# A top-32 attention and MLP kernel on one core: the first pair's steps spread over three PSUM banks, one weight product summed as the weights arrive, two pairs prepared in the MLP's bank, and a buffer for each chunk of rows

## The chip, the cores and the metric

The kernel runs on one core of a Trainium2 chip. A core has five engines that run side by side, each through its own queue in order: TensorE (PE, matrix products and transposes, writing to PSUM), VectorE (DVE), ScalarE (ACT), GpSimd (POOL) and SyncE (SP, which here issues nearly all DMAs). The metric is device time in microseconds. The kernel before took 906.09 us (median of three runs, 905.07 to 906.38).

## What is computed

```python
# 8 batches x 8 heads, 576 queries and keys, head size 64
scores = q @ k.T / 8
kth    = the 32nd largest score of the row
attn   = softmax(scores where scores >= kth, else -1e9)
x      = (attn @ v), heads side by side      # 4608 tokens x 512
h      = x @ w_in                             # 512 -> 2048
g      = max(h, 0) + alpha * min(h, 0)        # alpha per column
out    = g @ w_out                            # 2048 -> 512
```

The last three lines are computed as `relu(h) @ (w_out * (1 - alpha)) + x @ (w_in @ (w_out * alpha))`. The second product, `w_in @ (w_out * alpha)`, is a 512 x 512 matrix that does not depend on x. The text calls it the linear matrix; it is made once, on the chip, in the opening of the kernel.

## The kernel before

**Pairs, tiles, ticks.** Two heads of one batch form a pair; there are 32 pairs, four to a batch. Each pair has nine tiles of 128 rows of scores (the ninth holds the last 64 rows of both heads), 288 tiles in all. One Python loop writes the order of all engines by hand, tick by tick; tick n starts tile n. Within a tick each engine gets its instructions in a fixed order, and every engine runs its own list in order. So the engines drift apart, and wait on each other only through data and buffers.

**What a tile goes through.** PE makes scores (`ps`, line 319) one or two ticks ahead. ACT shifts them by the row's threshold guess (`b`, 328), takes a row sum of signs (`h`, 334) and later exponentials (`e`, 339). POOL turns the row sum into a sign bit (`SG`, 344). DVE then flips the tile (`y`, 350), takes six times the eight largest of a segment (`C`, 360), merges them (375, 377), and seven ticks after the tile began compares (`mk`, 424). POOL multiplies (`w`, 434; for the last six tiles DVE does both, 431). SP transposes the weights of two tiles by DMA (`wT`, 447; `wm` in 442 and 443 for ninth tiles), PE multiplies with v (`pu`, 493), DVE takes reciprocals (`rz`, 510) and ACT writes the rows to `xb` (522). In the last batch tiles run across the four pairs, and `av_last`, `rz_last` and `out_last` (493, 539, 546, the last two on DVE) take that place, three ticks after the weights, or two once all tiles have begun.

**Preparing a pair.** `prep_plan(p)` lays out steps at ticks counted from `BASE[p]`: transposes of q and k (`pq`, `pk`, and `pt` for the last 64 rows), a Gram matrix of k (`pg`), its product with q (`pr`, in two pieces of 512 and 64 columns), a product on DVE (`P`, 231), row statistics (`st`), and eight small DVE steps that give the threshold guess `NT0`. Before, `pq`, `pk`, `pt` and `pg` all take turns in one PSUM bank (`ps_a`), so each waits until ACT has copied the one before. `pr`, `st` and the `pu` of the attention product share the two banks of `ps_d`, which are handed out in rotation. Pairs 11 and 20 (`LEAD1`, `LEAD2`) are prepared early, four or five ticks beside another pair.

**Weights and MLP.** `weight_steps` gives PE and ACT one step per tick from tick 0: the rows of w_out are loaded and scaled (595, 596), then, in twelve steps at ticks 35 to 46, four 128 x 512 slices of the linear matrix are summed (`pl`, 603), six, six and four products to a slice, and copied (607). The bank is `ps_m`. When four chunks of `xb` and the chunk `xm` of a batch are written, SP transposes them (`xT`, 556 and 558), and `mlp_steps` feeds blocks of up to 512 tokens: `ph` (644), relu on ACT (650), `pz` (658, 662), copy (667), store (673). The blocks use `ps_m` too; between two feeds there are ticks with no MLP step. `xb` of a batch is one tile of four chunks in a single buffer.

**What sets the order at the end.** In the last batch up to two MLP steps are taken in a tick. After `av_last` of a chunk's second half the chunk is transposed, and its block is fed one tick later.

Of the kernel before, what the change touches and what calls it, by code (L numbers as in the profile page):

```python
# [9 lines left out]
FP32 = mybir.dt.float32  # L10
BF16 = mybir.dt.bfloat16
# [19 lines left out]
def kernel(  # L31
# [10 lines left out]
    nc = tc.nc  # L42
    B, H, S_, D = q.shape
# [7 lines left out]
    TPP = 9  # L51
# [118 lines left out]
    def prep_plan(p):  # L170
        d = pairs[p]
        GK = GKs[p % 2]
        ns = slice(p * TPP, p * TPP + TPP)

        def high(x):
            return x.bitcast(BF16).rearrange("p (n h) -> p n h", h=2)[:, :, 1]

        def pe_q():
            d["qkT"] = qkTs[p % NQ]
            d["pq"] = ps_a.tile([128, 512], FP32, name="pq", tag="pa")  # L180
            for c in range(4):
                nc.tensor.transpose(d["pq"][:, c * 128:(c + 1) * 128], d["q"][:, c, :], ident_f)

# [4 lines left out]
            nc.scalar.copy(d["v"][:, :, 0:D], d["st_v"])  # L188

        def pe_k():  # L190
            d["pk"] = ps_a.tile([128, 512], FP32, name="pk", tag="pa")
            for c in range(4):
                nc.tensor.transpose(d["pk"][:, c * 128:(c + 1) * 128], d["k"][:, c, 1:129],
                                    ident_f)
# [2 lines left out]
            nc.scalar.copy(d["qkT"][:, 1, 0:512], d["pk"])  # L197

        def pe_t():
            d["pt"] = ps_a.tile([128, 2, 64], FP32, name="pt", tag="pa")  # L200
            nc.tensor.transpose(d["pt"][:, 0, :], d["q"][0:64, 4, :], ident_f[0:64, 0:64])
            nc.tensor.transpose(d["pt"][:, 1, :], d["k"][0:64, 4, 1:129], ident_f[0:64, 0:64])

# [1 line left out]
            nc.scalar.copy(d["qkT"][:, :, 512:S], d["pt"])  # L205

        def pe_g():
            d["pg"] = ps_a.tile([128, 130], FP32, name="pg", tag="pa")
            for c in range(5):
                nc.tensor.matmul(d["pg"], high(d["k"][:, c, 1:129]), high(d["k"][:, c, :]),  # L210
                                 start=(c == 0), stop=(c == 4))
# [4 lines left out]
        def pe_r():  # L216
            d["P"] = prep.tile([128, S], BF16, name="P", bufs=1)
            d["pr"] = []
            d["qTb"] = high(d["qkT"][:, 0, :])
            for n0, n1 in ((0, 512), (512, S)):  # L220
                pr = ps_d.tile([128, n1 - n0], FP32, name="pr", tag="pd")
                for r in (slice(0, 64), slice(64, 128)):
                    nc.tensor.matmul(pr[r], GK[r, 1 + r.start:65 + r.start], d["qTb"][r, n0:n1],
                                     start=True, stop=True)
                d["pr"].append((n0, n1, pr))
# [5 lines left out]
                nc.vector.tensor_tensor(d["P"][:, n0:n1], pr, d["qkT"][:, 0, n0:n1], ALU.mult)  # L231

        def pe_s():
            st = ps_d.tile([128, 2, TPP], FP32, name="st", tag="pd")
# [49 lines left out]
        if p == 0:  # L284
            ts = [-16, -15, -14, -13, -12, -11, -9, -8, -8, -8, -8, -8, -8, -8, -8, -8, -2]
        elif p == 1:
            ts = [-9, -8, -7, -6, -5, -4, -3, -2, -2, -2, -2, -2, -2, -2, -1, -1, 1]
        else:
            ts = [-14, -13, -12, -11, -10, -9, -7, -6, -6, -5, -5, -4, -4, -3, -3, -2, -8]
# [3 lines left out]
                 dict(dve=[dve_p]), dict(pe=[pe_s]), dict(act=[act_m]), {dvx: [dve_2]},  # L293
                 dict(dve=[dve_3]), {dvx: [dve_4]}, dict(dve=[dve_5]), {dvx: [dve_6]},
                 dict(dve=[dve_7]), {dvx: [dve_8]}, dict(dve=[dve_9]), dict(act=[act_v])]
        return list(zip(ts, steps))

    tiles = {}
# [186 lines left out]

    def x_tiles(b):
        if b not in xb:
            xb[b] = prep.tile([128, 4, DM], BF16, name="xb", bufs=1)
            xm[b] = prep.tile([64, DM], BF16, name="xm", bufs=1)

    def av_one(o_, d, wT, side, cs):
# [22 lines left out]
    def av_out(p, g):  # L514
        d = pairs[p]
        b, kt = p // KPB, p % KPB
        pu, rz = d["pu", g], d["rz", g]
        for c in range(4 + 2 * g):
            m = 128 if c < 4 else 64
            h0 = 128 * kt + 64 * (c % 2)  # L520
            dst = xb[b][:, 2 * g + c // 2, h0:h0 + 64] if c < 4 else xm[b][:, h0:h0 + 64]
            nc.scalar.activation(dst, pu[0:m, c, 0:D], AF.Copy, scale=rz[0:m, c:c + 1])  # L522

    pul = {}
# [17 lines left out]
    def out_last(i, g):  # L542
        m = 128 if i < 4 else 64
        pu, rz = pul.pop((i, g))
        dst = xb[B - 1][:, i, :] if i < 4 else xm[B - 1]
        nc.vector.tensor_tensor(  # L546
            dst[:, 256 * g:256 * g + 256].rearrange("p (s d) -> p s d", s=4), pu[0:m, :, 0:D],
            rz[0:m, 0:4].unsqueeze(2).to_broadcast([m, 4, D]), ALU.mult)

    def x_turn(b, chunks):  # L550
        for i in chunks:
            c0 = (b * S + 128 * i) % NX
            if b == B - 1:
                c0 = b * S % NX + (64 + 128 * i if i < 4 else 0)
            if i < 4:
                nc.sync.dma_start_transpose(xT[:, :, c0:c0 + 128], xb[b][:, i, :])
            else:
                nc.sync.dma_start_transpose(xT[:, :, c0:c0 + 64], xm[b])

    def weight_steps():  # L560
# [17 lines left out]
        def lin(f):  # L578
            return xT[:, f // 4, DM * (f % 4):DM * (f % 4 + 1)]
# [15 lines left out]
            nc.scalar.activation(w_out_b[:, f, :], ws, AF.Copy, scale=alpha1m[:, f:f + 1])  # L595
            nc.scalar.activation(lin(f), ws, AF.Copy, scale=alpha_sb[:, f:f + 1])

        def w_id(kk, part):
            if part == 0:
                hold["pl"] = ps_m.tile([128, DM], FP32, name="pl", tag="misc")  # L600
            pl = hold["pl"]
            for f in range(6 * part, min(6 * part + 6, NFT)):
                nc.tensor.matmul(pl, hold["inT"][:, kk, f, :], lin(f),
                                 start=(f == 0), stop=(f == NFT - 1))

        def w_id2(kk):
            nc.scalar.copy(w_id_b[:, kk, :], hold["pl"])

        yield alpha, None
        yield (lambda: None), None  # L610
# [1 line left out]
        for f in range(NFT):  # L612
            yield ((lambda f=f: (w_out(f + 2) if f + 2 < NFT else None,
                                 w_in(f // 2) if f < 8 and f % 2 == 0 else None)),
                   (lambda f=f: w_out2(f)))
            yield (lambda: None), (lambda f=f: w_in2(f // 2) if f < 8 and f % 2 == 1 else None)
        for kk in range(NKT):
            for part in range(3):
                yield ((lambda kk=kk, part=part: w_id(kk, part)),
                       (lambda kk=kk: w_id2(kk)) if part == 2 else None)  # L620

    banks = [0, 0]

# [74 lines left out]
    with tc.manual_schedule(engines={E.PE, E.Activation, E.DVE, E.Pool, E.SP}):  # L698
# [19 lines left out]
        def tail_of(n, wn):  # L718
            wp, wj = ORDER[wn]
            b = wp // KPB  # L720
            if wp < P0:
                if wj == 3:
                    put(n + 3, "pe", lambda: av(wp, 0))
                    put(n + 4, "dve", lambda: av_rz(wp, 0))
                    put(n + 6, "act", lambda: av_out(wp, 0))
                    if wp % KPB == KPB - 1 and b >= 5:
                        put(n + 6, "end", lambda: x_turn(b, (0, 1)))
                        put(n + 8, "end", lambda: feed(b * S + 256))
                if wj == 8:
                    put(n + 4, "pe", lambda: av(wp, 1))  # L730
                    put(n + 5, "dve", lambda: av_rz(wp, 1))
                    put(n + 7, "act", lambda: av_out(wp, 1))
                    if wp % KPB == KPB - 1:
                        put(n + 7, "end", lambda: x_turn(b, range(2 if b >= 5 else 0, 5)))
                        put(n + 9, "end", lambda: feed((b + 1) * S))
            elif (wj == 8 or wj % 2) and wp % 2:
                i, g = wj // 2, (wp - P0) // 2
                dt = 3 if n < NT else 2
                put(n + dt, "pe", lambda: av_last(i, g))
                put(n + dt + 1, "dve", lambda: rz_last(i, g))  # L740
                put(n + dt + 1, "dvx", lambda: out_last(i, g))
# [247 lines left out]
```

## Time and profile before

| what | value |
|---|---|
| median of 3 runs | 906.09 us |
| profiled execution, its own time | 906.11 us |
| its span, first to last instruction | 904.2 us |
| DVE busy | 845.1 us (93%) |
| ACT busy | 787.6 us (87%) |
| PE busy | 737.7 us (82%) |
| POOL busy | 430.8 us (48%) |
| mean granted TensorE clock | 0.901 |

The shares are means over the whole run. A row of the timeline gives the start, the length, the engine, the line, and in brackets how long the engine stood idle before it and what released it. Lines are those of the kernel before; a queue of DMA issues is written with a q (SPq).

### The profile page before, as it was taken

How to read it: one execution, taken by the hardware profiler on the slowest of the kernel's cores; microseconds unless marked ns; L12 is line 12 of the kernel's file. 1: busy time of each engine (PE TensorE's matmuls, PEld its weight loads, DVE VectorE, ACT ScalarE, POOL GpSimd, SP SyncE). 2: the span in 40 equal slices, each digit the busy share in tenths (PEclk: the TensorE clock that was granted, in tenths of full speed). 3: DMA queues.
4: the chain of work that ended last, by engine and by line, in shares of the span. 5: the costliest groups of instructions: out<-in, count | busy, mean ns of one | idle time of the engine just before them, and what ended most of it. 6: DMA issues, size and time to landing. Idle time of an engine off the chain costs nothing. (4 is left out here: it accounts for less than half of the span.)

```text
span 904.2 us, 20676 instructions
## 1 busy us (share of the span) xinstructions
PE 737.7 (82%) x5747; PEld 433.0 (48%) x5747; DVE 845.1 (93%) x5305; ACT 787.6 (87%) x1809; POOL 430.8 (48%) x629
## 2 busy tenths in 40 slices
PE   5667697878958789887985879978897979899976
PEld 3344444434534445544453445644455555556663
DVE  3999989999998999999998999999999999989980
ACT  5999989799977998989996999999997999879831
POOL 1465544555454555554544555455545555445510
PEclk9665779699977999989996999999997999899989
DMA  6799644544665454564566445575455663444551
GB/s 153 135 176 205 128 81 90 118 92 93 139 130 95 94 105 114 100 134 89 109 150 112 91 94 112 109 142 92 97 118 105 123 108 87 81 88 88 91 99 33
DMA packets 343019, 99.50 MB, mean 110 GB/s; under 512 B 335200, under 2 KB 335216, under 8 KB 342896
## 3 DMA queue, kind: packets, MB, share of 16 engines
q1 hardware_dynamic: 340544, 95.71, 53.6%
q0 software_dynamic: 1152, 2.10, 1.7%
q8 instruction: 47, 0.77, 0.4%
q14 instruction: 76, 0.62, 0.2%
q10 hardware_dynamic: 1200, 0.30, 0.2%
HBM read 36.71 MB, written 9.44 MB: 51 GB/s over the span
## 5 line engine op out<-in xcount | busy, mean ns | idle before, releaser
L434 POOL TENSOR_TENSOR w<-mk,e 128x576 bf16<-128x576 bf16 x250 | 319.2, 1277 | 360.1 <-DVE mk L424 185.1
L360 DVE MAX8 C<-y 128x8 f32<-128x96 f32 x1728 | 420.5, 244 | 0.1
L319 PE MATMUL ps<-qkT 64*128 64x288 f32 (+1 forms) x1280 | 258.8, 478 | 34.8 <-ACT b L328 34.8
L328 ACT ACTIVATE b<-ps,NT 128x576 f32<-128x576 f32 x288 | 201.8, 758 | 19.3 <-PE ps L319 19.3
L334 ACT ACTIVATE h<-b 128x576 bf16<-128x576 f32 x288 | 202.7, 704 | 1.6
L644 PE MATMUL ph<-xT,w_in_b 128*128 128x128 bf16 (+2 forms) x1088 | 161.8, 299 | 44.7 <-ACT gT L650 34.1
L319 PEld LDWEIGHTS ps<-qkT 64*128 64x128 f32 (+1 forms) x1280 | 136.1, 195 | 96.5 <-ACT b L328 57.7
L339 ACT ACTIVATE e<-b 128x1152 bf16<-128x1152 f32 (+1 forms) x158 | 173.8, 1100 | 0.6 <-POOL w L434 0.6
L375 DVE MAX8 L<-C 128x8 f32<-128x48 f32 x864 | 163.4, 189 | 0.1
L350 DVE TENSOR_SCALAR y<-b,SG 128x576 int32<-128x576 int32 x288 | 147.3, 512 | 6.2 <-POOL SG L344 5.7
L424 DVE TENSOR_SCALAR mk<-b,KP 128x576 bf16<-128x576 f32 x282 | 143.8, 510 | 0.0
L644 PEld LDWEIGHTS <-w_in_b 128*128 128x128 bf16 x1088 | 87.9, 103 | 112.4 <-issue 81.5
L662 PE MATMUL pz<-w_out_b,gT 128*128 128x512 bf16 x576 | 139.6, 380 | 0.0
L650 ACT ACTIVATE gT<-ph 128x512 bf16<-128x512 f32 x144 | 87.9, 618 | 42.1 <-PE ph L644 42.0
L377 DVE MATCH_REPLACE8 C<-L,C 128x48 f32<-128x48 f32 x576 | 108.9, 189 | 0.0
L493 PE MATMUL pu<-v_bf,wT 128*128 128x65 bf16 (+1 forms) x1600 | 70.5, 200 | 29.7 <-DVE P L231 16.9
L493 PEld LDWEIGHTS <-wT 128*128 128x128 bf16 (+1 forms) x1600 | 66.1, 104 | 42.7 <-issue 20.5
L662 PEld LDWEIGHTS <-gT 128*128 128x128 bf16 x576 | 52.8, 98 | 69.2 <-issue 14.0
L344 POOL TENSOR_SCALAR SG<-S_all 128x1 int32<-128x1 f32 x288 | 65.2, 227 | 19.6 <-ACT h L334 19.6
L434 POOL TENSOR_TENSOR wm<-mk,e 128x576 bf16<-128x576 bf16 x32 | 40.8, 1276 | 52.1 <-DVE mk L424 46.6
L334 ACT ACTIVATION_READ_ACCUMULATOR h<-b 128x1 f32 x288 | 62.6, 217 | 0.0
L522 ACT ACTIVATE xb<-pu,rz 128x64 bf16<-128x64 f32 x224 | 53.9, 358 | 3.4 <-DVE C L360 2.5
(100 smaller groups left out, 716.0 us busy)
## 6 DMA issues: line engine op xcount, KB each, us to landing
out_dram<-o_sb SPq DMA_DIRECT2D x35, 256.0 KB, 2.3
st_q<-in_q_dram SPq DMA_DIRECT2D x64, 128.0 KB, 2.9
st_v<-in_v_dram SPq DMA_DIRECT2D x64, 128.0 KB, 2.6
kst<-in_k_dram SPq DMA_DIRECT2D x62, 128.0 KB, 2.8
w_stage<-in_moe_w_out_dram SPq DMA_DIRECT2D x16, 256.0 KB, 3.2
w_in_b<-in_moe_w_in_dram POOLq DMA_DIRECT2D x8, 256.0 KB, 6.6
wT<-w SPq DMA_TRANSPOSE x128, 3.3
st_q<-in_q_dram SPq DMA_DIRECT2D x32, 32.0 KB, 2.8
```

The lines of the kernel that those rows point to most:

```text
L319: nc.tensor.matmul(o_, l_, r_, start=True, stop=True)
L328: nc.scalar.activation(t["b"].rearrange("p (a c) -> p a c", a=2), t["ps"], AF.Identity, bias=NT0[:, p * TPP + j:p * TPP + j + 1], scale=ON ...
L334: nc.scalar.activation(h, tiles[n]["b"], AF.Sign, accum_out=S_all[:, n:n + 1])
L339: nc.scalar.activation(e, tiles[n0]["bu"], AF.Exp, scale=scl)
L350: nc.vector.tensor_scalar(t["y"].bitcast(I32), t["b"].bitcast(I32), FLIP, SG[:, n:n + 1], ALU.bitwise_xor, ALU.bitwise_xor)
L360: return [lambda g=g: nc.vector.max(out=C[:, n % TPP, g, :], in_=t["y"][:, g * SEG:(g + 1) * SEG]) for g in range(NSEG)]
L375: ops.append(lambda r=r, src=src: nc.vector.max(out=L[:, 8 * r:8 * r + 8], in_=src))
L424: nc.vector.tensor_scalar(t["mk"], t["b"], row_limit(n), None, ALU.is_ge)
L434: nc.gpsimd.tensor_tensor(dst, t["mk"], t["e"], ALU.mult)
L493: nc.tensor.matmul(o_, wT[:, 4 * side + c, cs], d["v"][:, 5 * side + c, :], start=(c == 0), stop=(c == 4))
L644: nc.tensor.matmul(hold[f][:, i, :], w_in_b[:, kk, (f + i) * 128:(f + i + 1) * 128], xT[:, kk, c0:c0 + tb], start=(kk == 0), stop=(kk == N ...
L662: nc.tensor.matmul(pz[0:m], hold["gT"][:, f, r0:r0 + m], w_out_b[:, f, :], start=False, stop=(f == NFT - 1))
```

## The change

- In `prep_plan`, a function `bank` now picks the PSUM pool by pair and step. For pair 0, `pq` and `pk` stay in `ps_a`, `pg` goes to `ps_m`, `pt` to `ps_d`. For pairs 11 and 20 all but the second piece of `pr` and `st` go to `ps_m`. For all other pairs nothing moves.
- For pair 0 the steps are regrouped: `pq`, `pg`, `pt` are issued together, their three copies follow, then `pr`, then `pk`; scores still come last.
- The first slice of the linear matrix is summed two products at a time between the weight loads, from step 6 on; one product is left for tick 35. The other three slices take four steps of four products. That is one step more in all, ending at tick 47.
- `xb` becomes four tiles of one chunk each in a rotation of six buffers.
- In the last batch the attention product follows the weights by two ticks throughout. Its rz and out_last, the transpose of the chunk and the feeding of its block move with it.

No operation is added or removed. On PE, DVE, ACT and SP some change places.

```diff
+        def bank(nm, shape):
+            pool, tag = (ps_d, "pd") if nm in ("pr1", "st") else (ps_a, "pa")
+            if nm == "pr0":
+                pool, tag = ps_d, "pd"
+            if p == 0 and nm == "pt":
+                pool, tag = ps_d, "pd"
+            if (p == 0 and nm == "pg") or (p in (LEAD1, LEAD2) and nm not in ("pr1", "st")):
+                pool, tag = ps_m, "misc"
+            return pool.tile(shape, FP32, name=nm, tag=tag)
...
-            d["pq"] = ps_a.tile([128, 512], FP32, name="pq", tag="pa")
+            d["pq"] = bank("pq", [128, 512])
...
-                pr = ps_d.tile([128, n1 - n0], FP32, name="pr", tag="pd")
+                pr = bank(f"pr{n0 // 512}", [128, n1 - n0])
...
+        if p == 0:
+            ts = [-16, -15, -14, -13, -12] + [-11] * 8 + [-2]
+            steps = [dict(pe=[pe_q, pe_g, pe_t]), dict(act=[act_q, act_g, act_t], pe=[pe_r, pe_k]),
+                     dict(dve=[dve_p]), dict(act=[act_k], pe=[pe_s]), dict(act=[act_m])] + steps[8:]
...
-            xb[b] = prep.tile([128, 4, DM], BF16, name="xb", bufs=1)
+            xb[b] = [prep.tile([128, DM], BF16, name="xb", bufs=6) for _ in range(4)]
...
-        def w_id(kk, part):
-            if part == 0:
-                hold["pl"] = ps_m.tile([128, DM], FP32, name="pl", tag="misc")
-            pl = hold["pl"]
-            for f in range(6 * part, min(6 * part + 6, NFT)):
-                nc.tensor.matmul(pl, hold["inT"][:, kk, f, :], lin(f),
+        done = [0]
+
+        def w_id(kk, lim):
+            if done[0] == 0:
+                hold["pl", kk] = ps_m.tile([128, DM], FP32, name="pl", tag="misc")
+            for f in range(done[0], lim):
+                nc.tensor.matmul(hold["pl", kk], hold["inT"][:, kk, f, :], lin(f),
                                  start=(f == 0), stop=(f == NFT - 1))
+            done[0] = lim % NFT
...
-            yield (lambda: None), (lambda f=f: w_in2(f // 2) if f < 8 and f % 2 == 1 else None)
-        for kk in range(NKT):
-            for part in range(3):
-                yield ((lambda kk=kk, part=part: w_id(kk, part)),
-                       (lambda kk=kk: w_id2(kk)) if part == 2 else None)
+            yield ((lambda f=f: w_id(0, min(done[0] + 2, f)) if f >= 6 else None),
+                   (lambda f=f: w_in2(f // 2) if f < 8 and f % 2 == 1 else None))
+        yield (lambda: w_id(0, NFT)), (lambda: w_id2(0))
+        for kk in range(1, NKT):
+            for lim in (4, 8, 12, 16):
+                yield ((lambda kk=kk, lim=lim: w_id(kk, lim)),
+                       (lambda kk=kk: w_id2(kk)) if lim == NFT else None)
...
                 i, g = wj // 2, (wp - P0) // 2
-                dt = 3 if n < NT else 2
+                dt = 2
                 put(n + dt, "pe", lambda: av_last(i, g))
```

More of the change, by code (lines that the diff above doesn't have):

```diff
@@ L190, in pe_k @@
         def pe_k():
-            d["pk"] = ps_a.tile([128, 512], FP32, name="pk", tag="pa")
+            d["pk"] = bank("pk", [128, 512])
             for c in range(4):
@@ L199, in pe_t @@
         def pe_t():
-            d["pt"] = ps_a.tile([128, 2, 64], FP32, name="pt", tag="pa")
+            d["pt"] = bank("pt", [128, 2, 64])
             nc.tensor.transpose(d["pt"][:, 0, :], d["q"][0:64, 4, :], ident_f[0:64, 0:64])
@@ L207, in pe_g @@
         def pe_g():
-            d["pg"] = ps_a.tile([128, 130], FP32, name="pg", tag="pa")
+            d["pg"] = bank("pg", [128, 130])
             for c in range(5):
@@ L233, in pe_s @@
         def pe_s():
-            st = ps_d.tile([128, 2, TPP], FP32, name="st", tag="pd")
+            st = bank("st", [128, 2, TPP])
             d["st"] = st
@@ L282, in dve_9 @@
                                     ALU.bitwise_or)
-        if p == 0:
-            ts = [-16, -15, -14, -13, -12, -11, -9, -8, -8, -8, -8, -8, -8, -8, -8, -8, -2]
-        elif p == 1:
+        if p == 1:
             ts = [-9, -8, -7, -6, -5, -4, -3, -2, -2, -2, -2, -2, -2, -2, -1, -1, 1]
@@ L520, in av_out @@
             h0 = 128 * kt + 64 * (c % 2)
-            dst = xb[b][:, 2 * g + c // 2, h0:h0 + 64] if c < 4 else xm[b][:, h0:h0 + 64]
+            dst = xb[b][2 * g + c // 2][:, h0:h0 + 64] if c < 4 else xm[b][:, h0:h0 + 64]
             nc.scalar.activation(dst, pu[0:m, c, 0:D], AF.Copy, scale=rz[0:m, c:c + 1])
@@ L544, in out_last @@
         pu, rz = pul.pop((i, g))
-        dst = xb[B - 1][:, i, :] if i < 4 else xm[B - 1]
+        dst = xb[B - 1][i] if i < 4 else xm[B - 1]
         nc.vector.tensor_tensor(
@@ L555, in x_turn @@
             if i < 4:
-                nc.sync.dma_start_transpose(xT[:, :, c0:c0 + 128], xb[b][:, i, :])
+                nc.sync.dma_start_transpose(xT[:, :, c0:c0 + 128], xb[b][i])
             else:
@@ L596, in w_out2 @@
             nc.scalar.activation(lin(f), ws, AF.Copy, scale=alpha_sb[:, f:f + 1])
-        def w_id(kk, part):
-            if part == 0:
-                hold["pl"] = ps_m.tile([128, DM], FP32, name="pl", tag="misc")
-            pl = hold["pl"]
-            for f in range(6 * part, min(6 * part + 6, NFT)):
-                nc.tensor.matmul(pl, hold["inT"][:, kk, f, :], lin(f),
+        done = [0]
[4 more added lines that the diff above has]
+                nc.tensor.matmul(hold["pl", kk], hold["inT"][:, kk, f, :], lin(f),
                                  start=(f == 0), stop=(f == NFT - 1))
+            done[0] = lim % NFT
         def w_id2(kk):
-            nc.scalar.copy(w_id_b[:, kk, :], hold["pl"])
+            nc.scalar.copy(w_id_b[:, kk, :], hold["pl", kk])
         yield alpha, None
```

## The prediction

> **What bounds the kernel now.** I read the page's busy times first, then what DVE waited for, then the timeline around each of those waits, then the clock granted to PE.
>
> ```profile
> PE 737.7 (82%) x5747; PEld 433.0 (48%) x5747; DVE 845.1 (93%) x5305; ACT 787.6 (87%) x1809; POOL 430.8 (48%) x629
> ```
>
> DVE is busy for 845.1 of 904.2 us, so at most 59.1 us can be won without touching DVE's work. The second view lists what ended DVE's idle time (total, times, longest):
>
> ```profile
> DVE P L231 <- PE pr L223: 6.1, 5, 3.8
> DVE sq L256 <- ACT MM L252: 3.7, 4, 1.2
> DVE xb L546 <- DMA xT<-xb: 3.4, 1, 3.4
> DVE rz L510 <- PE pu L493: 3.3, 3, 1.2
> ```
>
> Each is a handful of single stalls, not a rate. The table by stretches says what holds in between (length; then PE, PEld, DVE, ACT, POOL busy; clock; DMA):
>
> ```profile
> 60.00:80.00 20.00, 14.03 (x89) 9.27 (x88) 20.00 (x125) 19.91 (x48) 10.27 (x14) 0.66 1.06 187
> ```
>
> DVE runs without a gap and ACT nearly so, while PE has 6 of 20 us free. So I count only what shortens the opening, a DVE stall, or the end. The sum is made against the profiled execution, 906.11 us (span 904.2 and 1.9 around it), which equals the median of 906.09.
>
> **First pair.** These rows carry the chain up to the first `b`:
>
> ```profile
> 1.91 0.70 ACTq L138 DMA_DIRECT2D kst<-in_k_dram  x1
> 6.28 0.59 ACT L185 COPY qkT<-pq 128x512 f32<-128x512 f32 x1 [3.48 <-PE pq L182]
> 6.91 1.12 PE L193 MATMUL pk<-ident_f,kst 128*128 128x128 f32 x4 [0.68 <-ACT qkT L185]
> 9.53 0.70 PE L210 MATMUL pg<-kst 128*128 128x130 bf16 x5 [0.35 <-ACT qkT L205]
> 10.27 0.28 ACT L214 ACTIVATE GK<-pg 128x130 bf16<-128x130 f32 x1 [0.79 <-PE pg L210]
> 10.60 0.69 PE L223 MATMUL pr<-qkT,GK 64*64 64x512 bf16 x4 [0.37 <-ACT GK L214]
> 11.29 0.82 DVE L231 TENSOR_TENSOR P<-pr,qkT 128x512 bf16<-128x512 f32 x2 [0.46 <-PE pr L223]
> 12.54 2.29 PE L319 MATMUL ps<-qkT 64*128 64x288 f32 x8
> 12.83 0.73 ACT L188 CAST v_bf<-st_v 128x640 bf16<-128x640 f32 x1
> 14.87 1.37 ACT L328 ACTIVATE b<-ps,NT 128x576 f32<-128x576 f32 x2 [1.31 <-PE ps L319]
> ...
> kst<-in_k_dram ACTq DMA_DIRECT2D x1, 32.0 KB, 4.3
> ```
>
> Before, one bank makes `pq`, copy, `pk`, copy, `pt`, copy, `pg`, `GK`, `pr` a single line. After, `pg` (0.70) and `pt` run on PE while ACT copies `pq` (6.28 to 6.87): `pg` is done near 6.95, `GK` (0.28) near 7.25, `pr` (0.69) near 7.95, `P` (0.82) near 8.8. `pk` (1.12) stands behind `pr`, ends near 9.1, and its copy (0.59) near 9.7. Scores start there instead of at 12.54, so the first `b` moves by about 2.8. The last piece of k, issued at 1.91 and landing 4.3 later, is there at 6.2, in time. One cover may fail: the cast of v stands before `b` on ACT and is only known to be ready at 12.83. If it is not ready sooner, `b` starts at 13.56 and the gain is 1.3. The SP queue issues at the same pace as before, so the loads move up less than the work. I take 2.5, nearer the upper end since the chain's own rows give it; ends 1.3 and 2.8.
>
> **Linear matrix.** Around the fifth pair, in tick 35:
>
> ```profile
> 118.25 2.29 PE L319 MATMUL ps<-qkT 64*128 64x288 f32 x6 [0.54 <-ACT b L328]
> 120.47 2.74 PE L603 MATMUL pl<-xT,w_inT 128*128 128x512 bf16 x6
> 123.14 0.69 PE L223 MATMUL pr<-qkT,GK 64*64 64x512 bf16 x4
> 123.82 0.82 DVE L231 TENSOR_TENSOR P<-pr,qkT 128x512 bf16<-128x512 f32 x2 [3.83 <-PE pr L223]
> ```
>
> Six `pl` products stand before `pr`, and DVE waits 3.83 for `pr`. After, one product stands there. Five of six times 2.74 is 2.3, so I take 2.2; DVE then still waits about 1.6, for the scores ahead. The ends are 1.1 (half, if ACT holds those scores longer) and 3.8 (all of it). The fifteen products that went ahead cost 0.46 each, 6.9 us of PE in ticks 16 to 34, which the free PE time of the row for 60 to 80 hides; I cost them at nothing. If that cover were gone they would cost up to 6.9. The extra step at tick 47 ends before the first block of the MLP, and the later slices, four products a step, only thin PE out. Both count nothing.
>
> **Pairs 11 and 20.** Each leaves the same pattern:
>
> ```profile
> 270.47 1.26 PE L493 MATMUL pu<-v_bf,wT 128*128 128x65 bf16 x20 [6.51 <-DVE P L231]
> 271.77 0.18 DVE L510 RECIPROCAL rz<-pu 128x4 f32<-128x4 f32 x1 [1.22 <-PE pu L493]
> 273.98 1.37 ACT L328 ACTIVATE b<-ps,NT 128x576 f32<-128x576 f32 x2 [7.87 <-PE ps L319]
> 282.04 0.17 DVE L256 TENSOR_TENSOR sq<-MM 128x9 f32<-128x9 f32 x1 [1.21 <-ACT MM L252]
> ...
> 484.80 1.26 PE L493 MATMUL pu<-v_bf,wT 128*128 128x65 bf16 x20 [5.78 <-DVE P L231]
> 486.10 0.18 DVE L510 RECIPROCAL rz<-pu 128x4 f32<-128x4 f32 x1 [1.22 <-PE pu L493]
> 496.38 0.17 DVE L256 TENSOR_TENSOR sq<-MM 128x9 f32<-128x9 f32 x1 [1.22 <-ACT MM L252]
> ```
>
> Both pieces of `pr` sit in the two banks of `ps_d`, so the next `pu` must wait until DVE has made `P`. PE stands still for 6.51 and 5.78 us, everything queued behind (scores above all) is late, ACT starves for 7.87, and DVE pays twice: 1.22 for `rz`, 1.21 for `sq`. After, the first piece is in the MLP's bank and `pu` gets the bank of an earlier product, already copied out. The MLP's bank is free there: at one step a tick, the block fed at tick 51 ends at tick 80 and the next starts at tick 88, around ticks 81 to 86 of pair 11; for pair 20 it is 152 and 160 around 153 to 158. The same steps gain nothing from the new bank themselves. So 2.4 goes at each pair. If only the `rz` stall goes, 1.2 each; DVE has little more to give than 2.4, with perhaps 0.8 at pair 11 from smaller waits that follow. What would be late next is `pu`'s own transposed weights.
>
> **Chunk buffers, one tick less, and the end.**
>
> ```profile
> 783.71 2.92 PE L319 MATMUL ps<-qkT 64*128 64x288 f32 x8 [2.78 <-ACT b L328]
> 805.09 0.43 DVE L546 TENSOR_TENSOR xb<-pu,rz 128x256 bf16<-128x256 f32 x1 [3.39 <-DMA xT<-xb]
> 810.35 0.21 ACT L334 ACTIVATION_READ_ACCUMULATOR h<-b 128x1 f32 x1
> 813.03 0.51 DVE L350 TENSOR_SCALAR y<-b,SG 128x576 int32<-128x576 int32 x1
> 867.30 2.97 PE L662 MATMUL pz<-w_out_b,gT 128*128 128x512 bf16 x13
> 871.34 0.25 DVE L360 MAX8 C<-y 128x8 f32<-128x96 f32 x1
> 873.05 0.42 DVE L546 TENSOR_TENSOR xb<-pu,rz 128x256 bf16<-128x256 f32 x1
> 876.00 6.61 PE L644 MATMUL ph<-xT,w_in_b 128*128 128x128 bf16 x64 [2.94 <-DMA xT<-xb]
> 885.47 0.80 PE L493 MATMUL pu<-v_bf,wT 128*128 128x65 bf16 x20
> 890.03 3.75 PE L644 MATMUL ph<-xT,w_in_b 128*128 128x128 bf16 x64 [2.35 <-DMA xT<-xb]
> 894.48 3.62 PE L662 MATMUL pz<-w_out_b,gT 128*128 128x512 bf16 x16
> ...
> 878.00:880.00 2.00, 2.00 (x21) 2.00 (x20) 0.00 (x0) 0.95 (x2) 0.00 (x0) 0.50 1.09 205
> ```
>
> The wait of 3.39 goes: the last batch's first chunk gets a buffer that batch 5 left. But not all of it is won. The flip `y` at 813.03 needs row sums that ACT finishes at 810.56, 2.5 earlier. DVE may catch up by that, less some 0.5 for POOL's sign step (an estimate), so by 1.9; ACT and PE do not move.
>
> For the last but one block, `xb` no longer comes after three more merges but right after the `C` that ends at 871.59. It ends near 872.1 instead of 873.47, and 1.9 less is 870.2. `ph` began 2.53 after that instruction, so at 872.7 now. PE empties its queue at 870.27 and idles 2.4, close to the 2.35 that left the clock alone before the last `ph`. Then `ph` and all 20 `pz` take 8.07 (890.03 to 898.10), and a `pu` that moves in between 0.65. The last `pu` starts near 881.4, 4.1 earlier than 885.47. From its end to the last `ph` pass 3.76 (886.27 to 890.03). Six `pz` products filled part of that; now PE has nothing. I expect half clock after it, as after the 2.94: 6.61 instead of 3.75, plus 2.9. A store now stands before the last `xT` on SP, 0.2. So the end gives 1.0. Ends: 3.6 lost (DVE not ahead at all, both `ph` at half clock) and 5 won (neither at half clock, DVE further ahead). The other products moved up a tick cost nothing as long as their transposed weights are there; PE is busy with MLP work in this stage, which covers them.
>
> The Trainium skill, "TensorE: Matmul & The Clock Gate", Part 1 (The HAM clock gate), says that one idle window of about 3.4 us halves the clock and about 3.4 us of sustained work restores it, in windows that run freely. Here the half clock lasted from 876 to about 882, longer than one such window. By the page the last `ph` would lose an estimated 1.5 rather than 2.9, and the sum would be 894.2.
>
> **Sum.** 2.5 + 2.2 + 2.4 + 2.4 + 1.0 = 10.5, and 906.11 less 10.5 is 895.6.
>
> **Rivals.**
> - Both of the last blocks run at full clock: 2.9 less, 892.7 (889.5 to 893.5). For it: the gap of 2.35 stayed warm. Against: 2.78 before 783.71 did not, `ps` took 2.92 there.
> - The saved waits partly come back. ACT is as full as DVE in 60 to 80, so DVE may catch up with it. With the near ends (1.3, 1.1, 1.2, 1.2) and 1.7 lost at the end (both `ph` at half clock, DVE 1.9 ahead) that is 3.1 won, 903.0; around it 898.5 to 904.
> - The change does nothing measurable, 904.3 to 907.9: every stall is replaced by the next engine's. Against: PE and ACT were stalled by the same two waits.
> - Slower: in the last batch each `pu` is a tick earlier and PE runs in order. If these wait for `wT` by some 2.8 us each, the clock halves in the busiest PE stage. Half clock adds 0.76 to each us of full-clock work (6.61 against 3.75). To turn 10.5 won into 1.8 lost takes 12.3, so 16 us of work, a quarter of the stage from 805 to 870. At 20 us: 15.2 lost, 910.8.
>
> **How the numbers follow.** About 0.2% (1.8 us) can be told from no change. Forecast 0.56 (893.5 to 898.5), full clock 0.16, waits that come back 0.18, nothing 0.03, slower 0.07. The range 890 to 901.5 leaves out 0.02 of the full clock, 0.06 of the waits, and the last two: 0.18. Faster 0.90, same 0.03, slower 0.07.
>
> **What will show it.** The first `b` near 12.4; DVE's wait for `pr` near 120 at about 1.6; no PE wait for `P` of 6 us at pairs 11 and 20 and no `rz` stall after it; no DVE wait for `xT`; DVE idle down by some 11; the last `ph` about 6.6 long. I am wrong if ACT's `b` starts to wait where DVE was freed, if PE waits for `wT` in the last batch, or if the end moves by several us either way.

## The result, and the profile after

The changed kernel takes 894.11 us (median of 4 runs, 892.81 to 895.94) where the kernel before takes 905.92 beside it: a ratio of 0.9872, 95% interval 0.9852 to 0.9892, so 9.8 to 13.4 us less. The forecast was 895.6. The profiled execution took 893.49 us, its span is 891.6.

Busy times of the changed kernel, and what ended DVE's idle time (us in total, times, longest):

```profile
PE 734.1 (82%) x5747; PEld 429.3 (48%) x5747; DVE 844.7 (95%) x5305; ACT 788.4 (88%) x1809; POOL 430.9 (48%) x629
...
DVE P L241 <- PE pr L233: 2.4, 3, 1.5
DVE rz L522 <- PE pu L505: 2.0, 2, 1.7
DVE sq L266 <- ACT MM L262: 1.4, 2, 0.9
```

DVE's work is the same to 0.4 us (845.1 before); what went is its idle time, 59.1 before and 46.9 now. The wait of `xb` for `xT` is gone from the list, `P` waits 2.4 instead of 6.1, `sq` 1.4 instead of 3.7. The timeline of the first pair (start, length, engine, line):

```profile
5.16 1.09 PE L192 MATMUL pq<-ident_f,st_q 128*128 128x128 f32 x4 [5.16 <-DMA st_q<-in_q_dram]
6.03 0.75 PE L220 MATMUL pg<-kst 128*128 128x130 bf16 x5
6.82 0.28 ACT L224 ACTIVATE GK<-pg 128x130 bf16<-128x130 f32 x1
7.15 0.69 PE L233 MATMUL pr<-qkT,GK 64*64 64x512 bf16 x4
8.81 0.59 ACT L207 COPY qkT<-pk 128x512 f32<-128x512 f32 x1 [1.33 <-PE pk L203]
9.45 1.24 PE L331 MATMUL ps<-qkT 64*128 64x288 f32 x8 [0.34 <-ACT qkT L207]
11.76 0.73 ACT L198 CAST v_bf<-st_v 128x640 bf16<-128x640 f32 x1 [2.29 <-DMA st_v<-in_v_dram]
12.39 1.37 ACT L340 ACTIVATE b<-ps,NT 128x576 f32<-128x576 f32 x2
```

The first `b` starts at 12.39 instead of 14.87. The scores were done by 10.7; it is now the cast of v, waiting for its load, that holds `b`. Next, the same kernel in ticks 26 and 35, at pair 11, and at the end:

```profile
90.63 2.28 PE L331 MATMUL ps<-qkT 64*128 64x288 f32 x6 [2.59 <-ACT b L340]
92.85 0.61 PE L616 MATMUL pl<-xT,w_inT 128*128 128x512 bf16 x1
93.39 0.69 PE L233 MATMUL pr<-qkT,GK 64*64 64x512 bf16 x4
94.07 0.82 DVE L241 TENSOR_TENSOR P<-pr,qkT 128x512 bf16<-128x512 f32 x2 [1.48 <-PE pr L233]
...
119.17 0.61 PE L616 MATMUL pl<-xT,w_inT 128*128 128x512 bf16 x1
119.71 0.69 PE L233 MATMUL pr<-qkT,GK 64*64 64x512 bf16 x4
120.39 0.82 DVE L241 TENSOR_TENSOR P<-pr,qkT 128x512 bf16<-128x512 f32 x2 [0.43 <-PE pr L233]
...
261.98 0.73 PE L505 MATMUL pu<-v_bf,wT 128*128 128x65 bf16 x10 [0.69 <-DMA wT<-w]
...
861.47 3.26 PE L660 MATMUL ph<-xT,w_in_b 128*128 128x128 bf16 x32 [3.42 <-DMA xT<-xb]
871.59 0.80 PE L505 MATMUL pu<-v_bf,wT 128*128 128x65 bf16 x20
876.05 5.09 PE L660 MATMUL ph<-xT,w_in_b 128*128 128x128 bf16 x64 [2.65 <-DMA xT<-xb]
```

The wait for `pr` near 120 is 0.43 instead of 3.83, but a new one of 1.48 stands near 94, behind scores at half clock and one of the products moved ahead. At pair 11 `pu` no longer waits for `P`; it waits 0.69 for its transposed weights. At the end the block before last lost its clock (3.26 for its first half) and the last `ph` took 5.09.

To see where time goes I compare the flips `y` (L362, L350 before), of which there is one per tile: the shift of a tile is the start of its `y` in the first profile of before less its start in the other profile. The profiles of this document, one row each, in us, sorted by the parts that their kernels hold (`c_before` and `c_after` are the two kernels unchanged, profiled again; the others are explained with the experiments):

| kernel | tile 0 | 21 | 30 | 40 | 84 | 165 | 264 | 287 | span gained |
|---|---|---|---|---|---|---|---|---|---|
| c_before | -0.16 | 0.32 | -1.90 | -0.99 | -0.78 | 0.59 | 1.11 | 1.73 | 1.2 |
| e4_xb | -0.09 | -0.19 | -1.53 | -0.12 | 0.08 | 1.31 | 1.34 | 2.24 | 1.9 |
| e3_lead | -0.06 | -0.03 | -1.37 | -1.33 | -1.15 | 5.83 | 6.16 | 6.78 | 7.5 |
| e1_first | 2.52 | 2.39 | 0.64 | 1.77 | 1.97 | 1.42 | 0.96 | 1.54 | 2.1 |
| e2_lin | -0.15 | 0.34 | -1.91 | 0.18 | 0.36 | -0.75 | -1.22 | -0.64 | -0.1 |
| e10_nofirst | 0.20 | 0.06 | -3.26 | -1.14 | -1.01 | 6.09 | 6.07 | 7.31 | 6.8 |
| e6_nolin | 2.76 | 2.76 | -0.23 | 0.65 | 0.83 | 7.91 | 7.86 | 9.61 | 8.8 |
| e5_dt3 | 2.78 | 2.79 | -1.27 | 1.71 | 1.67 | 8.03 | 8.52 | 9.66 | 9.2 |
| after, first profile | 2.48 | 2.38 | 0.03 | 3.00 | 2.97 | 10.13 | 10.53 | 13.18 | 12.6 |
| c_after | 2.74 | 2.63 | -1.50 | 1.72 | 1.91 | 9.11 | 9.54 | 12.21 | 11.6 |
| e7_warm | 2.81 | 2.38 | -1.20 | 2.73 | 2.93 | 10.09 | 10.52 | 11.85 | 13.9 |
| e8_order | 2.62 | 2.20 | -1.77 | 2.16 | 2.35 | 9.54 | 9.39 | 11.32 | 14.2 |
| e9_best | 2.78 | 2.65 | -0.85 | 2.85 | 2.75 | 8.99 | 9.33 | 10.76 | 15.1 |

### The profile page after: what moved, and what is told of

Same layout as the page of the kernel before. It is cut to its first block, busy times and chain, and to the rows that moved or that the text cites. A ratio compares the mean times of both kernels' runs of the same rounds, so it can differ in the third digit from the quotient of the medians.

```text
span 891.6 us, 20671 instructions
## 1 busy us (share of the span) xinstructions
PE 734.1 (82%) x5747; PEld 429.3 (48%) x5747; DVE 844.7 (95%) x5305; ACT 788.4 (88%) x1809; POOL 430.9 (48%) x629
## 4 chain that ended last, share of the span: by engine, by line
DVE 66%; ACT 15%; PE 12%; DMA 4%; issue 1%; SPq 1%; POOL 1%; DVEq 0%; ACTq 0%
DVE C L372 21%; DVE y L362 10%; DVE mk L436 10%; DVE C L389 8%; DVE L L387 7%; ACT b L340 4%; ACT h L346 3%; PE ps L331 3%; PE pz L678 3%; ACT e L351 3%; PE ph L660 3%; DVE P L241 2%; DMA wT<-w 1%; PE pu L505 1%; DVE L L406 1%
## 5 line engine op out<-in xcount | busy, mean ns | idle before, releaser
L660 PE MATMUL ph<-xT,w_in_b 128*128 128x128 bf16 (+2 forms) x1088 | 159.4, 296 | 44.3 <-ACT gT L666 32.4
L331 PEld LDWEIGHTS ps<-qkT 64*128 64x128 f32 (+1 forms) x1280 | 134.0, 194 | 100.6 <-ACT b L340 62.7
L362 DVE TENSOR_SCALAR y<-b,SG 128x576 int32<-128x576 int32 x288 | 147.1, 511 | 7.5 <-POOL SG L356 6.8
L678 PEld LDWEIGHTS <-gT 128*128 128x128 bf16 x576 | 53.2, 98 | 70.7 <-issue 14.2
L446 POOL TENSOR_TENSOR wm<-mk,e 128x576 bf16<-128x576 bf16 x32 | 40.8, 1276 | 50.4 <-DVE mk L436 47.7
```

What stands on the lines that cost most here:

```text
L331: nc.tensor.matmul(o_, l_, r_, start=True, stop=True)
L362: nc.vector.tensor_scalar(t["y"].bitcast(I32), t["b"].bitcast(I32), FLIP, SG[:, n:n + 1], ALU.bitwise_xor, ALU.bitwise_xor)
L446: nc.gpsimd.tensor_tensor(dst, t["mk"], t["e"], ALU.mult)
L660: nc.tensor.matmul(hold[f][:, i, :], w_in_b[:, kk, (f + i) * 128:(f + i + 1) * 128], xT[:, kk, c0:c0 + tb], start=(kk == 0), stop=(kk == N ...
L678: nc.tensor.matmul(pz[0:m], hold["gT"][:, f, r0:r0 + m], w_out_b[:, f, :], start=False, stop=(f == NFT - 1))
```

## The experiments

**One part alone, four kernels on one chip.** Before took 906.07 there (29 runs, 902.36 to 909.32: the runs of this chip spread wider than the three at hand for the forecast). The first reading of the two profiles had suggested that the products moved ahead ate the start's gain, since at tile 30 of the first profile after nothing of it was left.

The first pair alone:

```diff
+            if p == 0 and nm == "pt":
+                pool, tag = ps_d, "pd"
+            if p == 0 and nm == "pg":
+                pool, tag = ps_m, "misc"
...
+            steps = [dict(pe=[pe_q, pe_g, pe_t]), dict(act=[act_q, act_g, act_t], pe=[pe_r, pe_k]),
```

> The kernel before with the first pair's new banks and order alone (three banks, its transposes and Gram product together). In the changed kernel the first flip `y` came 2.5 us earlier, and at tile 26 that lead was gone: 0.8 went at tile 22, where a product `pu` waited for its transposed weights, and 1.6 at tile 26, where DVE waited for `pr` behind a product `pl` that had been moved ahead. Theory (the start was won and the moved products ate it): without them 2.5 at tile 0, 1.7 left at tile 30 and at the end, 904.2 us. Rival (the opening is held by transfers and by ACT, whatever PE does): 2.5 at tile 0, nothing left at tile 30, 905.9 us, no difference.

Measured 904.03 us, ratio 0.9983 (0.9958 to 1.0007). The median is the theory's number, but the interval holds the rival's as well. At tile 30 the profile kept 0.64 of the lead, not 1.7, and the next kernels throw out the theory's reason.

The linear matrix alone:

```diff
+            yield ((lambda f=f: w_id(0, min(done[0] + 2, f)) if f >= 6 else None),
...
+        yield (lambda: w_id(0, NFT)), (lambda: w_id2(0))
```

> The kernel before with the linear matrix summed as the weights come, alone. Theory (the moved products cost 1.6 at tile 26 and win 3.4 at tile 35, less 0.4 at tile 37): 1.4 won, 904.5 us, DVE's wait for `pr` near 120 down from 3.83 to about 0.4, a new wait of DVE for `pr` near 96. Rival (the loss at tile 26 belongs to the earlier start, the products are free as forecast): 3.0 won, 902.9 us, and no new wait near 96.

Measured 906.07 us, ratio 0.9998 (0.9976 to 1.002): nothing, which neither had. The wait for `pr` near 124 fell to 1.60 only, there is no new wait near 96, and `rz` near 84 waits 3.06 (0.89 in the first profile of before).

Pairs 11 and 20 alone:

```diff
+            if p in (LEAD1, LEAD2) and nm not in ("pr1", "st"):
+                pool, tag = ps_m, "misc"
```

> The kernel before with pairs 11 and 20 in the MLP's bank, alone. Theory (each bank wait of PE costs DVE more than the two stalls that I counted: the changed kernel gained 3.6 at pair 11 and 2.6 at pair 20): 6.2 won, 899.7 us. Rival (only the two stalls, 1.22 and 1.21 at each pair; the rest came from the other parts): 4.8 won, 901.1 us. PE's waits of 6.51 and 5.78 for `P` are gone by both.

Measured 897.84 us, ratio 0.9917 (0.9895 to 0.9939), so 5.5 to 9.5 won: the theory's 6.2 and more, against 4.8 of the forecast. In two of the other single-part kernels, `e1_first` and `e2_lin`, pair 20, untouched, stalls longer than in the profile that the forecast was made on; in `e4_xb` it doesn't. Pair 20 in `e1_first`, DVE's waits:

```profile
482.71 0.18 DVE L522 RECIPROCAL rz<-pu 128x4 f32<-128x4 f32 x1 [1.22 <-PE pu L505]
494.04 0.17 DVE L266 TENSOR_TENSOR sq<-MM 128x9 f32<-128x9 f32 x1 [2.26 <-ACT MM L262]
497.53 0.82 DVE L241 TENSOR_TENSOR P<-pr,qkT 128x512 bf16<-128x512 f32 x2 [0.83 <-PE pr L233]
```

`sq` waits 2.26 here and 1.22 in the first profile, and the next `P` waits 0.83, which had no wait there.

The chunk buffers alone, with the tick as before:

```diff
-            xb[b] = prep.tile([128, 4, DM], BF16, name="xb", bufs=1)
+            xb[b] = [prep.tile([128, DM], BF16, name="xb", bufs=6) for _ in range(4)]
```

> The kernel before with a row buffer for each chunk, alone; the products of the last batch stay a tick later, as before. Theory (a wait of ACT for the old buffer at tile 134, 0.8, which I had not seen, and the whole 3.39 of DVE at the last batch, of which some 0.9 is given back in small waits): 3.3 won, 902.6 us; last `ph` at full clock, 3.75, since six `pz` products still stand close before it. Rival (what I forecast: nothing mid-run, and DVE keeps 1.9 of 3.39 as ACT's lead is only 2.5): 1.9 won, 904.0 us.

Measured 905.05 us, ratio 1.0005 (0.9981 to 1.0029): no difference shown. The 0.8 at tile 134 is won by the three kernels without the buffers too, so it is no effect of them. At the last batch 2.90 is won at tile 266 and 2.00 given back by tile 270, in waits for POOL's sign and for `pu`. And the opening, which this kernel doesn't touch, lags by 1.53 at tile 30.

**Both kernels a second time, and two edits of the end, on one chip** (before 908.44 there, 7 runs). The control, before unchanged:

> The kernel before, unchanged, profiled a second time. Theory (the one profile on which I predicted caught short waits by chance: in every single-part kernel the flips lag by 0.5 to 1.9 us at tile 30 against it, win 0.8 at tile 134, and two of three kernels with the old pairs lose 2.0 at pair 20): this profile shows the same against the first one, a lag of 1 to 2 us at tile 30, DVE waits at pair 20 of 4 us or more in place of 2.4. Rival (the lag comes from the edits): the same start times as in the first profile to 0.3 us.

Measured 904.80 us (one run). Its waits of DVE, then the SP queue and POOL ahead of the first of them:

```profile
84.62 0.18 DVE L510 RECIPROCAL rz<-pu 128x4 f32<-128x4 f32 x1 [3.11 <-PE pu L493]
124.82 0.82 DVE L231 TENSOR_TENSOR P<-pr,qkT 128x512 bf16<-128x512 f32 x2 [2.92 <-PE pr L223]
283.39 0.17 DVE L256 TENSOR_TENSOR sq<-MM 128x9 f32<-128x9 f32 x1 [1.79 <-ACT MM L252]
495.78 0.17 DVE L256 TENSOR_TENSOR sq<-MM 128x9 f32<-128x9 f32 x1 [1.21 <-ACT MM L252]
```

```profile
74.23 1.27 POOL L434 TENSOR_TENSOR w<-mk,e 128x576 bf16<-128x576 bf16 x1 [1.39 <-DVE mk L424]
76.01 1.89 SPq L587 DMA_TRANSPOSE w_inT<-w_in_b  x1
78.00 1.00 SPq L591 DMA_DIRECT2D w_stage<-in_moe_w_out_dram  x1
79.11 1.68 SPq L447 DMA_TRANSPOSE wT<-w  x1
83.84 0.73 PE L493 MATMUL pu<-v_bf,wT 128*128 128x65 bf16 x10 [6.44 <-DMA wT<-w]
```

The lag of 1.9 at tile 30 is there without any edit, as the theory had it; the 4 us at pair 20 are not (2.4 again). So the first profile was a quick one at tile 22: the attention weights `w` were ready at 75.50, but SP, which the transfers ahead of it keep busy without a gap, issues their transposition at 79.11, and `pu` starts at 83.84. How long this takes differs from run to run.

The changed kernel unchanged:

> The changed kernel, unchanged, on the chip of these runs. 894.1 us by the earlier runs. Theory: DVE's wait for `rz` near 81 and for `pr` near 94 changes by up to 1 us from profile to profile, while no wait of DVE stands at pairs 11 and 20 and none for `xT`. Rival: the same waits to 0.2 us.

Measured 894.84 us, ratio 0.9867 (0.9839 to 0.9895). DVE's wait for `rz` near 82 was 3.44 (1.67 in the first profile, so it moved by more than the 1 us expected), the one near 95 again 1.48, near 122 again 0.43; none stood at pairs 11 and 20, none for `xT`.

PE kept busy in its gaps at the end:

```diff
+                nd = {t7 + 320: 12, t7 + 448: 10}.get(t0, 0)
+                if nd:
+                    dm = ps_m.tile([128, DM], FP32, name="dm", tag="misc")
+                    for _ in range(nd):
+                        nc.tensor.matmul(dm, w_out_b[:, 0, 0:128], w_out_b[:, 0, :],
```

> The changed kernel with matrix products of no use (their result is read by nothing) on PE in its two idle gaps at the end: 12 ahead of the last block but one, 10 ahead of the last, each 128x512. Theory (idle PE loses its clock: `ph` of the two blocks took 5.2 and 5.1 us): both take 3.75, the last `pu` comes 1.5 to 1.9 earlier and the last `ph` is 1.3 shorter, 2.8 to 3.2 less, 891 us. Rival (the clock there is held down by something other than idleness, or the products themselves are in the way): both `ph` still over 5 us, or starting later, 894 us or more.

Measured 890.49 us, ratio 0.9800 (0.9771 to 0.9829). Its PE at the end:

```profile
859.21 2.75 PE L660 MATMUL dm<-w_out_b 128*128 128x512 bf16 x12
862.79 1.96 PE L666 MATMUL ph<-xT,w_in_b 128*128 128x128 bf16 x32 [0.83 <-DMA xT<-xb]
865.23 1.95 PE L666 MATMUL ph<-xT,w_in_b 128*128 128x128 bf16 x32
871.33 0.80 PE L505 MATMUL pu<-v_bf,wT 128*128 128x65 bf16 x20
873.90 2.32 PE L660 MATMUL dm<-w_out_b 128*128 128x512 bf16 x10 [0.75 <-DVE bad L495]
876.06 3.75 PE L666 MATMUL ph<-xT,w_in_b 128*128 128x128 bf16 x64
```

Both blocks run at full clock. From the last flip to the end it gains 2.66 on `c_after` (13.9 less 11.85, against 11.6 less 12.21), a little under the 2.8 expected. With PE kept busy the clock stayed up ahead of both blocks, so it was idleness that had cost it.

The last `pu` ahead of the `pz` before it:

```diff
-                dt = 2
+                dt = 1 if n == NT + 4 else 2
...
+            if n == NT + 5:
+                run(n, "pe")
             banks[0] = 2 if n >= NT else 1 if n >= N0 + 2 else 0
```

> The changed kernel with the last `pu` of all ahead of the twenty `pz` of the last block but one on PE, in place of behind them. Theory (the end is set by the order on PE: `pu` waited for nothing but `pz`): `pu` starts near 867.3 in place of 871.6, its turned rows arrive while `pz` runs, the last `ph` starts without a gap near 872.9 in place of 876.05 and takes 3.75 in place of 5.09: 4.4 less, 889.7 us. Rival (the last transposed weights land only behind `pz`): `pu` waits for them, `pz` is late by the same, 1 us won at most, 893 us.

Measured 891.33 us, ratio 0.9812 (0.9785 to 0.9839). Its PE, and the ACT step that PE waits for:

```profile
863.32 2.83 PE L660 MATMUL ph<-xT,w_in_b 128*128 128x128 bf16 x32 [3.41 <-DMA xT<-xb]
869.10 0.80 PE L505 MATMUL pu<-v_bf,wT 128*128 128x65 bf16 x20
870.60 3.62 PE L678 MATMUL pz<-w_out_b,gT 128*128 128x512 bf16 x16
874.05 1.95 PE L660 MATMUL ph<-xT,w_in_b 128*128 128x128 bf16 x32
877.62 1.95 PE L660 MATMUL ph<-xT,w_in_b 128*128 128x128 bf16 x32 [1.50 <-ACT gT L666]
...
876.97 1.09 ACT L666 ACTIVATE gT<-ph 128x512 bf16<-128x512 f32 x2 [2.13 <-DVE bad L495]
```

`pu` waits for nothing and the last `ph` follows `pz` at full clock. The end gains 3.49 on `c_after` (14.2 less 11.32), not 4.4: between the halves of `ph` PE stands 1.50 for ACT, which itself stood 2.13 for the closing flag `bad`.

**Parts taken away from the whole, and a version put together** (before 907.62 there, 9 runs). The tick given back:

```diff
-                dt = 2
+                dt = 3 if n < NT else 2
```

> The changed kernel without its one tick less: the products of the last batch stay where they were, all else as changed. By my forecast the end lost 0.9 by the earlier tick (2.9 and 0.2 lost, the rest won), so 893.6 us against 894.5 of the changed kernel. Theory now: the kernel with buffers and the old tick won 0.9 between tiles 264 and 287 and four with the new tick 1.3 to 2.7, so the old tick costs DVE 1.2 there, and the end is won by neither: 895.7 us. Both within what these rounds can just tell; the start times of the flips between tiles 264 and 287 tell more: 0.9 won by the theory now, 1.9 by the forecast.

Measured 894.21 us, ratio 0.9845 (0.982 to 0.987), not to be told from the changed kernel. Between tiles 264 and 287 it won 1.14, nearer to the theory's 0.9. Its last `ph`, with six `pz` close before it, took 5.36 after a gap of 2.35.

The linear matrix as before:

```diff
-            yield ((lambda f=f: w_id(0, min(done[0] + 2, f)) if f >= 6 else None),
+            yield (lambda: None), (lambda f=f: w_in2(f // 2) if f < 8 and f % 2 == 1 else None)
```

> The changed kernel with the linear matrix summed as before, all else as changed. By my forecast 2.2 is lost, 896.7 us, with DVE's wait for `pr` in tick 35 back at 3.8. Theory now: DVE's waits for `pr` near 94 and 121 together were 2.4 to 3.8 in five profiles without the early sum and 0.8 to 1.9 in five with it, so 1.9 lost, 896.4 us, but spread over both waits. Rival (alone, the part was worth 0.0): no difference, 894.5 us.

Measured 897.31 us, ratio 0.9883 (0.9862 to 0.9905), against 0.9867 and 0.9872 of the changed kernel: a loss of 1.0 to 1.5 by the ratios, inside their uncertainty, and 2.5 by medians of different chips. The wait near 123 is back, at 2.94, and there is none near 94.

The first pair as before:

```diff
-            steps = [dict(pe=[pe_q, pe_g, pe_t]), dict(act=[act_q, act_g, act_t], pe=[pe_r, pe_k]),
+        if p == 0:
+            ts = [-16, -15, -14, -13, -12, -11, -9, -8, -8, -8, -8, -8, -8, -8, -8, -8, -2]
```

> The changed kernel with the first pair as before, all else as changed. By my forecast 2.5 is lost, 897 us. Theory now (the lead of 2.5 is there at tile 0, but DVE then waits 1 to 2 longer at tiles 22 and 26 for transposed weights and `pr`, so that 0.6 to 1.6 of it remain at tile 40): 895.1 to 896.1 us. Rival (nothing of it remains): 894.5 us.

Measured 897.79 us, ratio 0.9878 (0.9849 to 0.9906), runs from 893.44 to 899.29. By the ratios that is 0.5 to 1.0 lost, inside their uncertainty. The profile, that of the slowest run, lags the kernels with all of the opening by 3.5 at tile 40; this fits the forecast's 2.5 better than the theory's 0.6 to 1.6, but one profile doesn't decide it.

The end put together, with the early products behind `pr`:

```diff
+            if n == NT + 5:
+                run(n, "pe")
...
+            while late:
+                late.pop(0)()
...
-                            put(n + 6, "end", final_flag)
+                            put(n + 5, "end", final_flag)
```

> The changed kernel with the last `pu` ahead of `pz`, the 12 products of no use ahead of the last block but one alone, the closing flag read one tick earlier (with the order changed, ACT had stood 0.8 for it and PE 1.5), and the early products of the linear matrix issued behind `pr` in their tick. Theory: the end wins 3.5 by the order, 1.5 by the flag, 0.7 to 1.5 by the clock, less what overlaps, 5.5; DVE's wait for `pr` near 94 falls from 1.3 to 0.9 at most: 888.5 us. Rival (the order already hides the cold `ph`, and the flag is waited for elsewhere): 891.3 us as with the order alone.

Measured 890.65 us (5 runs, 890.10 to 891.81), ratio 0.9816 (0.9798 to 0.9834). Its PE:

```profile
860.29 2.75 PE L662 MATMUL dm<-w_out_b 128*128 128x512 bf16 x12
863.87 1.96 PE L668 MATMUL ph<-xT,w_in_b 128*128 128x128 bf16 x32 [0.83 <-DMA xT<-xb]
874.80 3.75 PE L668 MATMUL ph<-xT,w_in_b 128*128 128x128 bf16 x64 [0.74 <-DVE bad L495]
```

The end gains 4.95 on `c_after`, near the 5.5 expected. The wait near 94 is 0.79, but it was 0.75 in `e7_warm`, whose early products stand ahead of `pr`, so what this order is worth is not shown. And its flips had 1.45 less of a lead at tile 287 than those of `c_after`, so that the time is no better than with the busy gaps alone. All three edits of the end beat the changed kernel; which is best can't be told.

## Why the prediction was right

The time was met because two terms that were off cancelled, and that was luck: the linear matrix won less than forecast, pairs 11 and 20 won more. I price each term from the table, as the mean of the profiles that hold a part less the mean of those that don't; several profiles on a side take out much of the scatter that fooled the first reading.

- **First pair: forecast 2.5.** `b` came at 12.39, forecast 12.4. The cover named as doubtful, the cast of v, is what ends last now. At tile 40 the start is worth 1.8 without the early sum (`e1_first` and `e6_nolin`, mean 1.21, against 0, -0.99, -1.33, -0.12) and 2.8 with it (six profiles, mean 2.36, against `e2_lin` and `e10_nofirst`, mean -0.48). The size is right, the path only in part. By the chain's own rows the scores would have ended near 12.0 (9.7 and 2.29); they ended at 10.7 to 11.9 in the eight profiles with the new start, as they ran at full clock in some. In all eight `b` follows the cast of v, which waits for its load, and starts at 12.06 to 12.39.
- **Linear matrix: forecast 2.2.** By the same four groups 0.1 without the new start, 1.15 with it; 0 to 1.5 by the ratios of the times. The step that failed is that the fifteen products moved ahead "cost nothing". DVE's waits, mean of six profiles without the early sum and eight with it (a wait not among those of 0.3 or more taken as 0):

| DVE waits | without | with |
|---|---|---|
| `rz` for `pu`, near 82 | 2.16 | 3.28 |
| `P` for `pr`, near 94 | 0.31 | 0.91 |
| `P` for `pr`, near 122 | 3.11 | 0.56 |

The wait that I priced fell by 2.55, as forecast. But 0.6 comes back near 94, and there the clock and the product both count. PE, then DVE, there in `e1_first`, which has no early product, and in `e2_lin`, which has one:

```profile
90.60 2.25 PE L331 MATMUL ps<-qkT 64*128 64x288 f32 x6 [2.59 <-ACT b L340]
92.78 0.69 PE L233 MATMUL pr<-qkT,GK 64*64 64x512 bf16 x4
93.46 0.82 DVE L241 TENSOR_TENSOR P<-pr,qkT 128x512 bf16<-128x512 f32 x2 [0.92 <-PE pr L233]
...
94.07 1.23 PE L327 MATMUL ps<-qkT 64*128 64x288 f32 x6 [2.55 <-ACT b L336]
95.24 0.39 PE L612 MATMUL pl<-xT,w_inT 128*128 128x512 bf16 x1
96.01 0.82 DVE L239 TENSOR_TENSOR P<-pr,qkT 128x512 bf16<-128x512 f32 x2
```

Where the scores ahead run at full clock (1.23 long) DVE doesn't wait, even with an early product in the way (`e2_lin`, `e10_nofirst`); where they take 2.25 or 2.29, at half clock, it waits 0.92 and 0.94 without any product (`e1_first`, `e4_xb`). With both it was 1.3 to 1.5 in four profiles; there `pr` begins 0.54 behind the product (92.85 and 93.39 in the changed kernel). So one early product cost about half a microsecond where the clock was low and nothing in the two profiles where it was full, and most of the rest goes with the clock. Not all of it: `e9_best` waited 0.79 behind scores of 1.32 with no product ahead of `pr`. The free PE time of the row for 60 to 80 was an average: in tick 26 PE stands idle 2.59 ahead of the scores and not at all from there to `pr`. Another 1.1 comes back near 82, behind SP's queue. There the single values overlap widely (0.89 to 3.88 without, 1.67 to 4.13 with), the products issue no transfer, and whether they cause it stays open.
- **Pairs 11 and 20: forecast 2.4 each, 4.8.** Between tiles 84 and 165 nine profiles with the new bank gained 6.94 on average, five without it 0.19: 6.75. The step that failed is the size: the two stalls of 1.2 were taken from one profile, as all that DVE had to give. The "0.8 more at pair 11", left out of the sum, is there each time: from tile 84 to 95 each of the nine gained 3.5, the five 0.3 on average, so 3.2. At pair 20 (tiles 140 to 165) the nine gained 2.6, while `e1_first` and `e2_lin` lost 2.0 there: `sq` waits 2.26 in both and the next `P` another 0.8 to 0.9. That makes 3.4 against the mean of the five, and why the old order stalls longer in some profiles stays open. The mechanism, and what comes next (`pu`'s own transposed weights), are as forecast.
- **Buffers, tick and end: forecast 1.0.** Between tiles 264 and 287 seven profiles with buffers and tick gained 1.86, five with neither 0.48: 1.4, where 1.9 was forecast from ACT's lead of 2.5. From the last flip to the end four with the new end (`after`, `c_after`, `e6_nolin`, `e10_nofirst`) lost 0.63 and five with neither part gained 0.26: 0.9 lost, as forecast (1.9 less 0.9). But the parts of that 0.9 were wrong. Ahead of the block before last PE stood idle 3.4, where the forecast had 2.4, and that block, forecast at full clock, lost its clock in all of these but `e10_nofirst`. The last `ph` lost 1.3 to 1.6 in three (1.34 in the first: 5.09 against 3.75), not 2.9; in `e10_nofirst` it took 6.43, 2.7 lost. The Trainium skill, "TensorE: Matmul & The Clock Gate", Part 1 (The HAM clock gate), gave an estimated 1.5 here, which the trace of the first three bears out.
- **Sum.** 2.36 and 0.61 for the opening make 3.0 (forecast 4.7), with 6.75 and 0.5 it is 10.2, inside the measured 9.8 to 13.4.

Of the rivals, "waits partly come back" is true of the opening in part and false of the pairs; "both blocks at full clock" took an extra edit; in the last batch PE didn't wait for `wT` as the slower case needed.

## What to carry to other kernels

A stall of a microsecond read from one profile has an error as large as itself: here the unchanged kernel moved by 1.9 us at one tile from profile to profile, and a second profile of each kernel showed at once which steps belong to the edit. PE time that is free on average is not free in the tick where a chain passes through PE: here one product ahead of `pr` cost half a microsecond where the clock was low. Filler behind the chain's own instruction would avoid that, though no run here shows its worth. At the end of a kernel, an in-order queue is worth reading backwards: the last `pu` stood behind 4.3 us of products that nobody waited for, and moving it, or filling the gaps, won more than the buffers did.

## What I had not expected of the hardware

Whether PE loses its clock in a gap does not follow from the gap's length alone. Before the last `ph` a gap of 2.35 to 2.37 left it at full clock in four profiles (3.75: the first of before, `e1_first`, `e2_lin`, `e3_lead`) and not in three (5.36: `c_before`, `e4_xb`, `e5_dt3`); a gap of 3.43 before the block before last left it at full clock in `e10_nofirst` (1.96 for 32). In `c_before` the clock fell only after `ph` had run for a microsecond (length; PE, PEld, DVE, ACT, POOL busy; clock; DMA):

```profile
886.00:887.00 1.00, 0.00 (x0) 0.10 (x1) 0.00 (x0) 0.00 (x0) 0.00 (x0) 1.00 0.58 212
887.00:888.00 1.00, 0.80 (x15) 0.77 (x15) 0.00 (x0) 0.00 (x0) 0.00 (x0) 1.00 0.17 59
888.00:889.00 1.00, 1.00 (x15) 1.00 (x13) 0.00 (x0) 0.60 (x1) 0.00 (x0) 0.60 0.00 0
...
891.00:892.00 1.00, 1.00 (x15) 1.00 (x14) 0.00 (x0) 0.36 (x1) 0.00 (x0) 0.70 0.00 0
```

Taking each row's clock as a mix of 1.00 and 0.50, the half clock lasted from about 888.2 to 891.6, 3.4 us. In every profile the granted clock changes in steps of 3.41 us or a multiple of it, so the time between can be divided into such steps, and PE's busy time in each can be read. In the step ahead of that drop, 884.79 to 888.20, PE worked for 1.04 of 3.41 us, 31%; in `e4_xb` and `e5_dt3` it was 31% and 32%. In the four profiles that kept the clock the same gap fell otherwise across the steps, and the emptiest step around it held 65% (the first of before), 45% (`e1_first`, `e2_lin`) and 41% (`e3_lead`). The gap of 3.43 in `e10_nofirst` was cut into two steps of 51% and 48%. Behind 855 us, in all fourteen profiles, each full-clock step with PE busy for up to 40.5% was followed by half clock, and none with 40.8% or more was. So at this end it is not the gap that counts but how it falls on the steps. It isn't the whole rule: ahead of 855 us, where other products run, steps with more than 60% were followed by half clock too.

The same page of the Trainium skill says that the windows of about 3.4 us run freely, which fits these steps and the chance in them; that the clock falls after a window that is idle doesn't fit to the letter, since PE had idled for only 2.37 us of the 3.41.
